# The second MLP of a fused attention-MLP kernel on one core: six token blocks of 384 columns in place of four of 512 and one of 256

## The chip, the core and the metric

The kernel runs on one core of one Trainium2 chip. The metric is device time in microseconds (us) of one execution; lower is better. TensorE (PE) does the matmuls and its weight loads (PEld), ScalarE (ACT) and VectorE (DVE) do the element-wise work, SyncE (SP) issues nearly all DMA transfers, GpSimd (POOL) a few.

## What is computed

Random-feature attention on 4 batches of 8 heads and 576 positions, then two MLPs on its 2304 tokens. The change touches the last one only.

```python
# x: [2304, 512], the attention's result after its heads are put side by side
a = x @ w_a                                   # w_a, w_b: [512, 1536]
b = x @ w_b
y = (a * b) @ w_out                           # w_out: [1536, 512]; first MLP
h = np.maximum(y @ w_in2, 0.0)                # w_in2: [512, 2048]; second MLP
out = (h * h) @ w_out2                        # w_out2: [2048, 512]
```

## The kernel before

**Numbers as two parts.** Every large matmul keeps fp32 accuracy by cutting each operand into a high part and a rest, both in the fp32r format. A product is then three matmuls, by the table `TERMS = ((0, 0), (0, 1), (1, 0))`: high by high, high by rest, rest by high. What an engine produces in fp32 is cut by one cast on ACT (the high part) and one subtraction on DVE (the rest).

**First MLP.** `a_units` goes over the tokens in 9 passes and over the hidden dimension in 12 slices of 128. While its passes run on PE, the attention of later tokens is done beside it (`SIDES`). The result of a pass, transposed (512 features in 4 chunks of 128 partitions, tokens along the free dimension), is scaled by ACT into a tile `y_s` (line 647) and stored to DRAM tensors `y_d`, one for each 512 tokens (line 649). The pool of `y_s` has two buffers.

**Weights of the second MLP.** 16 slices of 128 hidden features. `get_w2` loads one slice of `w_in2` and `w_out2` and cuts both (`split`, lines 151 to 175, some eight instructions on ACT and DVE for each slice). Thirteen slices come in during the last pass of the first MLP; the last three are cut in the first block of the second MLP, in tiles named `w2r`. All 16 then stay on the chip.

**Second MLP.** `BB` lists the token blocks: four of 512 and one of 256 columns. `b_units(i)` does one block. For each hidden slice `f`:

- PE: 12 matmuls `ph` (line 777; 4 chunks of the features by 3 terms) of 128 weights by the block's columns, `yx` streaming;
- ACT: `r` is the scaled relu of `ph` (line 784). DVE: `r` squared (line 785). ACT: the high part of `ss` (line 786). DVE: its rest (line 787);
- PE, one slice later: `outs(f - 1)`, for each tile of 128 tokens three matmuls that stream 512 columns of `w_out2`, with `ss` as the weights, into the bank `o` of that token tile (line 764). So `outs` is 12 matmuls for a block of 512 tokens.

I call `ph` of one slice and `outs` of one slice together a unit. After the last unit, ACT scales each `o` bank into a tile `o_s` (line 796), and SP stores it to the output (line 798). **The pool of `o_s` has two buffers** (line 955): the third `o_s` of a block waits until the store of the first has landed. The next block's relu `r` stands behind these `o_s` in ACT's queue.

`y_load(i)` brings the columns of block `i` back from `y_d`, one feature chunk at a time: a load into `yraw` (line 727; the two buffers of `y_s`), a cast (728) and a subtraction (729) into `yx`. `yx` has one buffer on either side of the memory, used by even and odd blocks, so the load of block `i + 2` can only fill `yx` after the last `ph` of block `i`.

The instructions of one engine run in a fixed order. It comes from the library's scheduler, which places each instruction when its own model of the chip says that the operands are there; the order in the source is only its input. So loads of a later block stand, in the program that runs, at the end of an earlier one.

Of the kernel before, what the change touches and what calls it, by code (L numbers as in the profile page):

```python
# [35 lines left out]
def f32(ap):  # L36
    return ap.bitcast(F32)
# [7 lines left out]
def kernel(  # L45
# [13 lines left out]
    nc = tc.nc  # L59
    B, H, S, D = q.shape  # L60
    M = omega.shape[0]
    NT, DM = out.shape
# [9 lines left out]
    N = 256  # L72
    NBLK = NT // N
# [30 lines left out]
    def bank(i, shape, name):  # L104
# [3 lines left out]
    y_d = [  # L108
        dram.tile([128, KC, min(2, NBLK - i) * N], F32, name=f"y_d{i // 2}")
        for i in range(0, NBLK, 2)  # L110
    ]
# [602 lines left out]

    wi2, wo2 = {}, {}

    BB = [(i * N, min(2, NBLK - i) * N) for i in range(0, NBLK, 2)]
    ys = {}
    op_pool = []

    def y_load(i, pool):
        w_ = BB[i][1]
        t = pool.tile([128, KC, 2, w_], F32R, tag="yx", name=f"yx{i}")
        ys[i] = t
        for c in range(KC):
            r = ypool.tile([128, w_], F32, tag="ys", name="yraw")
            nc.sync.dma_start(out=r, in_=y_d[i][:, c, :])
            nc.scalar.copy(out=t[:, c, 0, :], in_=r)
            nc.vector.tensor_tensor(
                out=t[:, c, 1, :], in0=r, in1=f32(t[:, c, 0, :]), op=ALU.subtract  # L730
            )
# [20 lines left out]
    def b_units(i):  # L752


        y = ys[i]
        c0, w_ = BB[i]
        s_t, op = {}, {}
# [100 lines left out]
    def get_w2():  # L858
        f = w2["n"]
        if f >= FB:  # L860
            return
        w2["n"] += 1
        if f < W2_L:
            po = (w2["l"], "w2")
        elif f < W2_L + FA:
            po = (wpool, "w")
        else:
            po = (w2["r"], "w2r")
        wi2[f], wo2[f] = get_pair(("b", f), 1, *po, (w_in2, f, False), (w_out2, f, True))
# [30 lines left out]
    side, n_side, done, u = iter(()), 0, 0, 0  # L900
# [18 lines left out]
    for pi, f, kind in a_units():  # L919
        _, f0, f1 = PASSES[pi]  # L920
        n_units = (f1 - f0) * 3
        step()
        if kind == "a":
            w_due += W_AT.get(pi, 0) / (f1 - f0)
            while (w_due > 0.999 or w_next <= f + 2 and w_next < f1) and w_next < FA:
                get_w(w_next)
                w_next += 1
                w_due -= 1
        if kind == "o" and (pi or f >= LAG):
            get_wo(n_wo)  # L930
            n_wo += 1
        if pi == last:
            if f == 0 and kind == "o":
                top["st"].close()
                open_split()

            if (f or kind == "o") and w2["n"] < W2_L + f + (kind != "a"):
                get_w2()
            if f == 4 and kind == "o":
                y_load(0, w2["yl"])  # L940
        u += 1
        while done < min(n_side, u * n_side / (n_units * FR.get(pi, 1.0))):
            next(side, None)
            done += 1
        if u == n_units and pi < last:
            begin(pi + 1)
# [8 lines left out]
    op_pool.append(ctx.enter_context(tc.tile_pool(name="op", bufs=2, side="right")))  # L955
    for i in range(len(BB)):
        for f in b_units(i):
            step()
            get_w2()
            if f == (4 if i == 0 else FB - 6) and i + 1 < len(BB):  # L960
                y_load(i + 1, w2["yl" if i % 2 else "yr"])
# [33 lines left out]
```

## Time and profile before

| | us |
|---|---|
| runs: median (lowest to highest) of 3 | 1052.88 (1050.69 to 1053.01) |
| the profiled execution's own time | 1052.61 |
| its span in the profile | 1050.8 |
| PE matmuls busy | 1024.0 (97% of the span) |
| DVE busy | 526.8 (50%) |
| ACT busy | 471.2 (45%) |
| share of PE in the chain that ended last | 88% |
| share of `o` (line 764) and `ph` (line 777) in that chain | 19% and 18% |

The span is what the profile's clock counts from the first to the last instruction; the execution's own time is 1.81 us longer. PE's busy time is built from modelled ends of pipelined matmuls, so a high share alone does not tell at which rate it works; the times from one group of matmuls to the next do.

### The profile page before, as it was taken

How to read it: one execution, taken by the hardware profiler on the slowest of the kernel's cores; microseconds unless marked ns; L12 is line 12 of the kernel's file. 1: busy time of each engine (PE TensorE's matmuls, PEld its weight loads, DVE VectorE, ACT ScalarE, POOL GpSimd, SP SyncE). 2: the span in 40 equal slices, each digit the busy share in tenths (PEclk: the TensorE clock that was granted, in tenths of full speed). 3: DMA queues.
4: the chain of work that ended last, by engine and by line, in shares of the span. 5: the costliest groups of instructions: out<-in, count | busy, mean ns of one | idle time of the engine just before them, and what ended most of it. 6: DMA issues, size and time to landing. Idle time of an engine off the chain costs nothing.

```text
span 1050.8 us, 14948 instructions
## 1 busy us (share of the span) xinstructions
PE 1024.0 (97%) x5641; PEld 873.6 (83%) x5641; DVE 526.8 (50%) x1274; ACT 471.2 (45%) x1079; POOL 28.9 (3%) x54
## 2 busy tenths in 40 slices
PE   4899999999999999999999999999999999999998
PEld 3789989999988877788888888788788888888887
DVE  4788885665654445444337987722222322322222
ACT  4887757554455443333326665522322322322232
POOL 3100101000000000000000000000000000000000
PEclk9999999999999999999999999999999999999999
DMA  6846864663432211312227664300200200100010
GB/s 166 242 148 205 267 233 120 210 209 95 142 105 80 63 46 56 95 62 70 66 87 264 230 220 174 107 1 0 81 1 1 71 1 1 51 1 1 0 41 21
DMA packets 83144, 105.90 MB, mean 101 GB/s; under 512 B 26240, under 2 KB 65152, under 8 KB 83072
## 3 DMA queue, kind: packets, MB, share of 16 engines
q1 hardware_dynamic: 81536, 103.37, 30.7%
q0 software_dynamic: 1536, 1.58, 0.5%
q8 instruction: 45, 0.74, 0.3%
q14 instruction: 27, 0.22, 0.1%
HBM read 87.62 MB, written 17.30 MB: 100 GB/s over the span
## 4 chain that ended last, share of the span: by engine, by line
PE 88%; DVE 4%; DMA 3%; ACT 3%; issue 1%; SPq 1%; ACTq 0%; DVEq 0%
PE abw L610 19%; PE o L764 19%; PE ph L777 18%; PE y L635 12%; PE ab L610 7%; PE ps_n L481 3%; PE ps_p L285 2%; PE ps_kv L423 2%; PE ps_p L351 2%; PE ps_qt L474 1%; DMA raw<-in_moe_w_out_dram 1%; PE ps_t L330 1%; DMA qn<-in_q_dram 1%; DVE p L159 1%; PE ps_x L492 1%
## 5 line engine op out<-in xcount | busy, mean ns | idle before, releaser
L635 PE MATMUL y<-gs,wo 128*128 128x256 f32 (+1 forms) x864 | 177.2, 345 | 0.0
L764 PE MATMUL o<-w,ss 128*128 128x512 f32 x702 | 170.9, 390 | 1.4 <-ACT ss L786 1.4
L777 PE MATMUL ph<-yx,w 128*128 128x512 f32 (+1 forms) x780 | 169.8, 368 | 0.0
L777 PEld LDWEIGHTS ph<-yx,w 128*128 128x128 f32 x780 | 137.4, 188 | 25.3
L785 DVE TENSOR_TENSOR r<-r 128x512 f32<-128x512 f32 (+1 forms) x80 | 51.1, 639 | 209.8 <-ACT r L784 209.8
L764 PEld LDWEIGHTS o<-w,ss 128*128 128x128 f32 x702 | 130.5, 188 | 29.7 <-ACT ss L786 2.2
L635 PEld LDWEIGHTS y<-gs,wo 128*128 128x128 f32 x864 | 136.6, 190 | 15.2
L610 PE MATMUL abw<-x_all,w 128*128 128x512 f32 x576 | 146.6, 398 | 0.0
L784 ACT ACTIVATE r<-ph 128x512 f32<-128x512 f32 (+1 forms) x80 | 44.5, 556 | 208.4 <-PE ph L777 208.2
L610 PE MATMUL ab<-x_all,w 128*128 128x256 f32 x864 | 132.9, 295 | 0.3 <-DVE x_all L549 0.2
L610 PEld LDWEIGHTS abw<-x_all,w 128*128 128x128 f32 x576 | 105.5, 189 | 19.2
L610 PEld LDWEIGHTS ab<-x_all,w 128*128 128x128 f32 x864 | 115.0, 193 | 1.5 <-DVE x_all L549 0.5
L787 DVE TENSOR_TENSOR ss<-r,ss 128x512 fp32r<-128x512 f32 (+1 forms) x80 | 51.1, 639 | 46.6 <-ACT ss L786 40.0
L610 PE MATMUL abw<-x_mid,w 128*128 128x512 f32 x288 | 73.1, 400 | 0.0
L786 ACT CAST ss<-r 128x512 fp32r<-128x512 f32 (+1 forms) x80 | 46.2, 577 | 51.5 <-DVE r L785 51.5
L610 PEld LDWEIGHTS abw<-x_mid,w 128*128 128x128 f32 x288 | 52.1, 189 | 9.8
L358 DVE CUSTOM_DVE_ANT_0 c<-ps_p,c 128x128 f32<-128x128 f32 x152 | 37.8, 287 | 32.5 <-ACT c L356 32.0
L701 ACT CAST gs<-a_s 128x256 fp32r<-128x256 f32 (+1 forms) x96 | 40.6, 433 | 28.3 <-DVE a_s L700 28.1
L164 DVE SCALAR_TENSOR_TENSOR raw<-raw 128x1024 uint32<-128x1024 uint32 (+1 forms) x40 | 42.5, 1062 | 13.4 <-ACT raw L152 13.3
L152 ACT ACTIVATE raw<-raw 128x1024 int32<-128x1024 uint16 (+1 forms) x40 | 40.8, 1020 | 11.4 <-DMA raw<-in_moe_w_out_dram 9.3
L702 DVE TENSOR_TENSOR gs<-a_s,gs 128x256 fp32r<-128x256 f32 (+1 forms) x96 | 42.8, 454 | 5.3 <-ACT gs L701 4.2
L151 ACT ACTIVATE a<-raw 128x1024 f32<-128x1024 f32 (+1 forms) x40 | 40.6, 1014 | 10.9 <-DMA raw<-in_moe_w_out_dram 5.6
(109 smaller groups left out, 1212.9 us busy)
## 6 DMA issues: line engine op xcount, KB each, us to landing
wo<-wo_d SPq DMA_DIRECT2D x60, 512.0 KB, 3.5
raw<-in_moe_w_out_dram SPq DMA_DIRECT2D x28, 512.0 KB, 4.8
raw<-in_moe_w_in_dram SPq DMA_DIRECT2D x16, 512.0 KB, 3.9
raw<-in_moe_w_a_dram SPq DMA_DIRECT2D x12, 512.0 KB, 4.8
raw<-in_moe_w_b_dram SPq DMA_DIRECT2D x12, 512.0 KB, 6.1
wo_d<-wo SPq DMA_DIRECT2D x12, 512.0 KB, 3.4
kn<-in_k_dram SPq DMA_DIRECT2D x16, 256.0 KB, 3.5
V<-in_v_dram SPq DMA_DIRECT2D x16, 256.0 KB, 3.4
```

Source lines behind the costliest of these rows:

```text
L151: nc.scalar.activation(out=a, in_=f32(up), func=ACTF.Copy, scale=WORD_SCALE)
L152: nc.scalar.activation(out=u, in_=raw.bitcast(U16)[:, :, :, 1], func=ACTF.Copy, scale=2.0 ** 7,)
L164: nc.vector.scalar_tensor_tensor(out=u.bitcast(U32), in0=up.bitcast(U32), scalar=23, in1=u.bitcast(U32), op0=ALU.logical_shift_left, op1=A ...
L610: nc.tensor.matmul(ps, lhsT=wv[:, s_, kc, :], rhs=x[..., kc, m_, :], start=(kc == 0 and (s_, m_) == TERMS[0]), stop=(kc == KC - 1 and (s_, ...
L635: nc.tensor.matmul(y_part(pi, f, c), lhsT=wo[pi, f][:, s_, c * 128:(c + 1) * 128], rhs=g[:, m_, :],  start=(f == f0 and (wide or c % 2 == ...
L702: nc.vector.tensor_tensor(out=g[:, 1, c], in0=a_s, in1=f32(g[:, 0, c]), op=ALU.subtract)
L764: nc.tensor.matmul(op[t], lhsT=s_t[f][:, s_, t * 128:(t + 1) * 128], rhs=wo2[f][:, m_, :], start=(f == 0 and (s_, m_) == TERMS[0]), stop=( ...
L777: nc.tensor.matmul(ps, lhsT=wv[:, s_, kc, :], rhs=y[:, kc, m_, :], start=(kc == 0 and (s_, m_) == TERMS[0]), stop=(kc == KC - 1 and (s_, m ...
L784: nc.scalar.activation(out=r, in_=ps, func=ACTF.Relu, scale=1.0 / W_SCALE)
L785: nc.vector.tensor_tensor(out=r, in0=r, in1=r, op=ALU.mult)
L786: nc.scalar.copy(out=s_t[f][:, 0, :], in_=r)
L787: nc.vector.tensor_tensor(out=s_t[f][:, 1, :], in0=r, in1=f32(s_t[f][:, 0, :]), op=ALU.subtract)
```

## The change

The list of blocks becomes six of 384 columns. Since the DRAM tensors `y_d` still hold 512 tokens each, a block's columns may lie in two of them, and its load is then made of two transfers. Nothing else in the source differs; the lines behind it move down by six (777 becomes 783, 796 becomes 802).

```diff
-    BB = [(i * N, min(2, NBLK - i) * N) for i in range(0, NBLK, 2)]
+    NB = 384
+    BB = [(c, NB) for c in range(0, NT, NB)]
...
             r = ypool.tile([128, w_], F32, tag="ys", name="yraw")
-            nc.sync.dma_start(out=r, in_=y_d[i][:, c, :])
+            done = 0
+            while done < w_:
+                d, o = divmod(BB[i][0] + done, 2 * N)
+                cnt = min(w_ - done, 2 * N - o)
+                nc.sync.dma_start(out=r[:, done:done + cnt], in_=y_d[d][:, c, o:o + cnt])
+                done += cnt
```

A block now has three token tiles, so `outs` is 9 matmuls and a unit 12 `ph` of 384 columns and 9 `o` of 512. There are 96 units, where there were 64 of the wide kind and 16 of the narrow kind.

**Where ACT's queue moves: between two blocks.** ACT at the end of the first block of the second MLP, before. Names carry buffer numbers; `o0` to `o3` are the banks of the four token tiles, `o_s` the scaled output tiles, `yx2` the input of the third block.

```order
L784 ACTIVATE r_7736<-ph_7723 128x512
L728 CAST yx2_8111<-yraw_8112 128x512
L728 CAST yx2_8111<-yraw_8116 128x512
L786 CAST ss_7737<-r_7736 128x512
L796 ACTIVATE o_s_7766<-o0_7249 128x512
L796 ACTIVATE o_s_7769<-o1_7253 128x512
L728 CAST yx2_8111<-yraw_8120 128x512
L728 CAST yx2_8111<-yraw_8124 128x512
L796 ACTIVATE o_s_7772<-o2_7257 128x512
L796 ACTIVATE o_s_7775<-o3_7261 128x512
```

The same place with the change.

```order
L790 ACTIVATE r_7697<-ph_7684 128x384
L734 CAST yx2_8032<-yraw_8033 128x384
L734 CAST yx2_8032<-yraw_8038 128x384
L792 CAST ss_7698<-r_7697 128x384
L802 ACTIVATE o_s_7721<-o0_7249 128x512
L802 ACTIVATE o_s_7724<-o1_7253 128x512
L734 CAST yx2_8032<-yraw_8043 128x384
L734 CAST yx2_8032<-yraw_8048 128x384
L802 ACTIVATE o_s_7727<-o2_7257 128x512
```

The fourth `o_s` is gone; the next row is, with the change as before, the next block's first relu. Two `yx` casts and a third `o_s` still stand ahead of it. This holds for the first four of the five places between blocks; at the fifth there are no `yx` casts.

**Where SP's queue moves: the loads.** SP with the change, from the first block's last `ph` on: the loads of `yx2` and the stores of the first two `o_s`. `y_d1` and `y_d2` are DRAM tensors of 512 tokens each.

```order
L732 DMA yraw_8043<-y_d1_98 128x256
L732 DMA yraw_8043<-y_d2_99 128x128
L732 DMA yraw_8048<-y_d1_98 128x256
L732 DMA yraw_8048<-y_d2_99 128x128
L804 DMA out_0_dram<-o_s_7721 128x512
L804 DMA out_0_dram<-o_s_7724 128x512
```

Before, one load of 128x512 stands for each of the two pairs. The block that is loaded at the first place comes in such pairs, and so does the one at the fourth place; at the second and the third each chunk is one load of 128x384.

**Where ACT's queue moves: the start of the second MLP.** Before (`y2`, `y3` are the last results of the first MLP, `w2r` and `raw` belong to weight splits):

```order
L647 ACTIVATE y_s_7179<-y2_6518 128x512
L163 CAST w2r_7226<-p_7266 128x2x512
L647 ACTIVATE y_s_7183<-y3_6519 128x512
L784 ACTIVATE r_7220<-ph_7207 128x512
L152 ACTIVATE raw_7276<-raw_7276 128x1024
L784 ACTIVATE r_7243<-ph_7230 128x512
L786 CAST ss_7221<-r_7220 128x512
```

With the change:

```order
L647 ACTIVATE y_s_7179<-y2_6518 128x512
L790 ACTIVATE r_7220<-ph_7207 128x384
L163 CAST w2r_7226<-p_7262 128x2x512
L647 ACTIVATE y_s_7183<-y3_6519 128x512
L792 CAST ss_7221<-r_7220 128x384
L790 ACTIVATE r_7243<-ph_7230 128x384
```

The first relu moved ahead of the cast of `w2r` and of the last `y_s`, and the first `ss` ahead of a step of a weight split. On PE, 31 matmuls `ph` stand ahead of the first `o` before, and 29 with the change.

## Rows read from the trace of the kernel before

**Rows 1.** Busy time by engine inside the second block; PEclk is the granted clock.

```profile
core 0: us, PE busy (x) PEld busy (x) DVE busy (x) ACT busy (x) POOL busy (x), PEclk, DMA share, GB/s
...
750.00:820.00 70.00, 70.00 (x311) 57.96 (x310) 18.04 (x26) 15.84 (x26) 0.00 (x0) 1.00 0.00 0
```

**Rows 2.** Chain that ended last: a unit of 512 columns (start us, us, what).

```profile
667.98 2.72 PE o L764 x12
670.70 2.72 PE ph L777 x12
```

**Rows 3.** The same chain: a unit of the block of 256 columns.

```profile
1014.43 1.43 PE ph L777 x12
1015.87 1.39 PE o L764 x6
```

**Rows 4.** Groups by shape, weight loads inside the block of 256 columns (busy us, mean ns).

```profile
L777 PEld LDWEIGHTS ph<-yx,w 128*128 128x128 f32 x109 | 14.3, 191 | 0.7
```

**Rows 5.** Groups by shape, ACT and DVE, the whole second MLP.

```profile
L785 DVE TENSOR_TENSOR r<-r 128x512 f32<-128x512 f32 x64 | 44.3, 693 | 184.0 <-ACT r L784 184.0
L784 ACT ACTIVATE r<-ph 128x512 f32<-128x512 f32 x64 | 38.3, 599 | 186.7 <-PE ph L777 186.7
L785 DVE TENSOR_TENSOR r<-r 128x256 f32<-128x256 f32 x16 | 6.8, 426 | 25.9 <-ACT r L784 25.9
L784 ACT ACTIVATE r<-ph 128x256 f32<-128x256 f32 x16 | 6.1, 384 | 21.7 <-PE ph L777 21.6
```

**Rows 6.** Timeline, start of the second MLP (start us, us, engine, line, what, count [idle before]).

```profile
650.26 7.19 PE L777 MATMUL ph<-yx,w 128*128 128x512 f32 x31
...
653.60 0.60 ACT L647 ACTIVATE y_s<-y 128x512 f32<-128x512 f32 x1 [1.32 <-DMA y_d<-y_s]
...
656.20 1.14 ACT L152 ACTIVATE raw<-raw 128x1024 int32<-128x1024 uint16 x1
...
658.38 3.02 PE L764 MATMUL o<-w,ss 128*128 128x512 f32 x12 [0.93 <-ACT ss L786]
```

**Rows 7.** Timeline, from the first to the second block: stores, loads and what waits.

```profile
733.10 5.78 PE L764 MATMUL o<-w2r,ss 128*128 128x512 f32 x24
...
737.08 1.09 ACT L796 ACTIVATE o_s<-o 128x512 f32<-128x512 f32 x2 [1.58 <-PE o L764]
737.70 1.71 SPq L798 DMA_DIRECT2D out_dram<-o_s  x2
...
738.72 5.60 PE L777 MATMUL ph<-yx,w 128*128 128x512 f32 x24
...
740.62 0.62 ACT L728 CAST yx<-yraw 128x512 fp32r<-128x512 f32 x1 [1.43 <-DMA yraw<-y_d]
...
741.79 1.09 ACT L796 ACTIVATE o_s<-o 128x512 f32<-128x512 f32 x2 [0.55 <-DMA out_dram<-o_s]
...
744.79 3.29 PE L764 MATMUL o<-w,ss 128*128 128x512 f32 x12 [0.48 <-ACT ss L786]
```

**Rows 8.** Timeline, the third place between blocks, whose loads are 128x256.

```profile
913.05 4.29 SPq L798 DMA_DIRECT2D out_dram<-o_s  x4
...
915.78 1.20 ACT L796 ACTIVATE o_s<-o 128x512 f32<-128x512 f32 x2 [0.28 <-DMA out_dram<-o_s]
```

**Rows 9.** Timeline, the fourth place, without loads.

```profile
995.89 5.63 PE L764 MATMUL o<-w2r,ss 128*128 128x512 f32 x24
...
999.50 1.29 ACT L796 ACTIVATE o_s<-o 128x512 f32<-128x512 f32 x2 [1.38 <-PE o L764]
1000.13 5.00 SPq L798 DMA_DIRECT2D out_dram<-o_s  x5
...
1002.25 0.60 ACT L796 ACTIVATE o_s<-o 128x512 f32<-128x512 f32 x1 [1.45 <-DMA out_dram<-o_s]
```

**Rows 10.** Timeline, the end of the program.

```profile
1043.90 3.26 PE L764 MATMUL o<-w2r,ss 128*128 128x512 f32 x12
...
1047.12 1.03 SPq L798 DMA_DIRECT2D out_dram<-o_s  x2
```

## The prediction, made before the changed kernel ran

> **What bounds the kernel now.** I read the chain that ended last first: it is PE for 88%, and from the start of the second MLP it shows nothing but `o` and `ph` in turn, 2.72 us for each group of 12 matmuls of 512 columns [rows 2]. That is 226.7 ns for one matmul. Next I asked whether anything else presses: inside a block PE is busy for 70.00 of 70.00 us at a granted clock of 1.00, which is the 2.4 GHz level, while DVE and ACT work 18.0 and 15.8 us of them and no bytes move [rows 1]. So inside a block PE's own pace is the bound, and everything else is covered. The timeline then shows where PE does wait: at the start of the second MLP [rows 6], and between blocks [rows 7 to 9]. The reader is to see in rows 7 that the third `o_s` waits for the first store to land, and that the next block's first `o` waits for what stands behind that `o_s` on ACT. The end of the program is a fixed tail: last matmuls, `o_s`, store [rows 10].
>
> So the change is costed in three parts: PE's work, PE's waits, the tail. I use the profiled execution: 1052.61 us, 0.27 below the median of the three runs; its span is 1050.8.
>
> **PE's work.** Before, a wide unit is 5.44 us [rows 2] and a narrow one 1.43 + 1.39 = 2.82 us [rows 3]; 64 of the one and 16 of the other make 348.2 + 45.1 = 393.3 us. With the change `outs` streams the same 512 columns for the same 18 token tiles, 864 matmuls as before: no saving. `ph` streams as many columns in all, in 96 × 12 = 1152 matmuls where there were 80 × 12 = 960. No row has 384 columns. The bounds are 119.2 ns for 256 columns [rows 3] and 226.7 ns for 512 [rows 2]; the two lie on a line of 2.4 columns to the nanosecond plus some 13 ns for each matmul, and its middle is 173 ns. A unit is then 12 × 173 + 9 × 226.7 ns = 4.12 us, 96 of them 395.1 us. Beside short groups an `o` group took 1.39 us for 6, which is 0.03 over the wide rate; half of that in each of 96 units would make 396.5. I take 395.5: **2.2 us more work**, between 1.8 and 3.2.
>
> A rule of the Trainium skill says how much a finer cut costs. The page "TensorE: Matmul & The Clock Gate", section Back-to-back issue gap, gives columns over 2.4 GHz plus about 2.5 ns as the gap of matmuls one behind another at the full clock. As an estimate from that page, 192 more matmuls would cost 0.5 us and the sum below would be 1.7 us lower. The trace does not agree, with some 13 ns over the columns' time at both sizes [rows 2, 3], and the sum goes by the trace.
>
> ACT and DVE do 96 small rounds instead of 80. At 384 columns I put `r` at 0.49 us and its square at 0.56, midway in rows 5, and the cast like `r`. One slice's chain, some 2.2 us, is covered by the `outs` and `ph` that lie between, 4.1 us. Cost nothing; without that cover it would be 2 us a unit.
>
> **PE's waits, before.** The first `ph` starts at 650.26 [rows 6] and the last matmul ends at 1043.90 + 3.26 = 1047.16 [rows 10]: 396.9 us for 393.3 of work, so 3.6 us of waits in all, 0.93 of it at the start [rows 6].
>
> **Waits between blocks.** Let T be the start of the last `outs` of a block. At the first place T = 733.10 + 2.72 = 735.82 [rows 7]. The first `o_s` starts at T + 1.26, its store is issued at T + 1.88, and the third `o_s` starts at T + 5.97, 4.09 us after the issue. From it to the next block's first `o` are 3.00 us, 0.49 of it the fourth `o_s` (two take 1.09, one 0.60). PE could have gone on at T + 2.72 + 5.44 = T + 8.16 and went on at T + 8.97.
>
> With the change PE comes to the same point earlier: T + 2.04 + 4.15 = T + 6.19. ACT's order is the same but for the fourth `o_s`. From the third `o_s` to the first `o` I count 3.00 − 0.49, less 0.11 + 0.13 + 0.11 for the shorter relu, square and cast [rows 5], which is 2.16 us. Let w be the time from the first store's issue to the third `o_s`. PE then waits 1.88 + w + 2.16 − 6.19 = w − 2.15 us. The rows give w = 4.09 beside loads of 512 columns [rows 7], 2.73 beside loads of 256 [rows 8], 2.12 beside none [rows 9]. For 384 columns I take the middle of the first two, 3.4, since load size orders these three: a wait of 1.3 us. That is for the second and third place.
>
> At the first and fourth place the loads come in two pieces. The last of them is issued two issues later, of some 0.5 us each [rows 10], and its cast stands ahead of the third `o_s`. Before, that cast began at T + 4.80 [rows 7]; about 0.9 later it ends near T + 6.2, and PE would wait 6.2 + 2.16 − 6.19 = 2.2 us. The smaller bytes pull the other way; I take 2.0. The fifth place has no loads: w = 2.12, no wait. Sum **6.6 us** (2 × 1.3 + 2 × 2.0). The ends: nothing, if w is 2.12 everywhere; 9.3, with 4.09 everywhere and 0.8 more for the pieces.
>
> **Waits at the start.** 29 `ph` take 5.0 us, so PE is done with them at 655.3, where 31 had taken it to 657.45 [rows 6]. The first `ss` now stands ahead of a split step of 1.14 us and of the second relu, 0.49; with the shorter relu and cast the first `o` comes at about 658.38 − 1.14 − 0.49 − 0.2 = 656.55. The wait is 1.3 us, for 0.93. After it ACT and DVE still owe the splits of two weight slices and the loads of the second block, at units that last 4.12 us instead of 5.44; I add 0.7 for this. Together 2.0, between 0.9 and 3.0. With 0.3 of remains, the waits come to 2.0 + 6.6 + 0.3 = 8.9, **5.3 more than before**.
>
> **The tail.** Before, the last block had two tiles for two `o_s` buffers, so nothing waited. Now its third `o_s` waits for its first store. From T of the last block: first `o_s` at T + 0.89 (999.50 less 995.89 + 2.72) and store at T + 1.52 [rows 9], landed 2.12 later, third `o_s` at T + 3.64, its store at T + 4.26. Before, the second store was issued at the end of the `o_s`, 3.0 us ahead of the span's end [rows 10]; so the span ends at T + 7.3, that is 5.2 us behind the last matmul (T + 2.04), where it was 1050.8 − 1047.16 = 3.6: **1.6 us more**, between 1.2 and 2.4.
>
> **Sum.** 1052.61 + 2.2 + 5.3 + 1.6 = 1061.7 us, 0.8% slower.
>
> **The rivals.**
>
> *The stores land undisturbed (no change).* With smaller loads and one `o_s` less, the first store might land 2.12 us after its issue at every place, as in rows 9. It decides at w = 2.15: below it ACT is ready before PE and the places between blocks cost nothing. If the start also stays at 0.93, the waits fall by 2.4 and the time is 1052.61 + 2.2 − 2.4 + 1.6 = 1054.0. For it: the one place without loads. Against it: w was over 2.7 at each of the places with loads [rows 7, 8], and four of five places still have them.
>
> *Weight loads set the pace of `ph`.* A load is 191 ns on average [rows 4] and a matmul of 384 columns would be 173. If loads bound it, 1152 × 18 ns = 20.7 us come on top: 1082.4. Against it: the same loads stand beside matmuls that follow each other every 119 ns [rows 3], so they overlap one another.
>
> *PE's clock falls behind longer waits.* The wait of 0.93 us [rows 6] and those between blocks left the clock at its upper level. Waits of 2 us or more could bring a stretch at 1.2 GHz, where a unit would take 8.24 us; one such unit behind each of four places costs 4 × 4.12 = 16.5 us: 1078.2. Nothing in the rows shows such a fall in this MLP. The Trainium skill's page "TensorE: Matmul & The Clock Gate", section Why this matters for your kernels, warns that pauses between bursts of matmuls bring back the half clock.
>
> **How the numbers follow.** The forecast has 0.87, the undisturbed stores 0.08, the weight loads 0.02, the clock 0.03. About 0.3% is what a measurement of this kernel can tell from no change, 3.2 us on 1052.88. The forecast's bounds: the places between blocks alone reach from 0 to 9.3 us around 6.6, work, start and tail add about 1 us to either side. Its likely part is 1056.5 to 1066.5; the first rival lies just below, the other two far above, and together they are less than 2 in 10, so the range stays at that. Slower by over 0.3% takes the forecast and the last two rivals, 0.92; no change takes the first rival, 0.07, and 0.01 of it is left for faster.
>
> **What would show each step.** In the changed profile: groups of 12 `ph` at 2.08 us (a group near 2.3 would mean weight loads); the first `o` of blocks two to five some 1.3 to 2 us late, with a third `o_s` that waits for the store just ahead of it, and the last block without that wait; the granted clock at 1.00 in every block; a third `o_s` at the end that starts about 2.1 us behind the first store. The prediction is wrong if PE goes from one block to the next without a wait, or if the waits between blocks exceed 3 us each.

## The result, and the profile after

| | before | with the change |
|---|---|---|
| median of 4 runs each, us (lowest to highest) | 1051.89 (1050.69 to 1053.01) | 1063.13 (1061.44 to 1065.62) |
| ratio to before, 95% interval | | 1.0109 (1.0082 to 1.0136) |
| profiled execution: own time / span, us | 1052.61 / 1050.8 | 1065.62 / 1063.8 |

The change costs 1.1%, within the range that was forecast. But two of its three terms were wrong, one far too small and one far too large, and they made up for each other. The profile shows which.

First the chain that ended last, inside the second block (start us, us, what); it answers to [rows 2].

```profile
740.35 2.10 PE ph L783 x12
742.45 2.08 PE o L770 x9
744.54 2.10 PE ph L783 x12
```

A unit is 4.19 us, where I had put 4.12. Now the busy times of the same block, which answer to [rows 1]:

```profile
core 0: us, PE busy (x) PEld busy (x) DVE busy (x) ACT busy (x) POOL busy (x), PEclk, DMA share, GB/s
735.00:780.00 45.00, 45.00 (x229) 40.85 (x228) 12.00 (x22) 10.56 (x21) 0.00 (x0) 1.00 0.00 1
```

PE shows no idle time there, and its clock is at the upper level, 2.4 GHz. So the 0.07 us lie between matmuls that follow each other without a wait. The timeline at the fourth place between blocks, which answers to [rows 7]:

```profile
919.25 4.44 PE L770 MATMUL o<-w2r,ss 128*128 128x512 f32 x18
...
921.27 0.54 PEld L770 LDWEIGHTS o<-w2r,ss 128*128 128x128 f32 x3 [0.22 <-ACT ss L792]
...
922.04 1.21 PEld L770 LDWEIGHTS o<-w2r,ss 128*128 128x128 f32 x6 [0.23 <-DVE ss L793]
922.59 1.09 ACT L802 ACTIVATE o_s<-o 128x512 f32<-128x512 f32 x2 [1.36 <-PE o L770]
923.21 4.07 SPq L804 DMA_DIRECT2D out_dram<-o_s  x3
923.52 4.35 PE L783 MATMUL ph<-yx,w 128*128 128x384 f32 x24
...
925.40 0.51 ACT L734 CAST yx<-yraw 128x384 fp32r<-128x384 f32 x1 [0.72 <-DMA yraw<-y_d]
...
926.32 0.60 ACT L802 ACTIVATE o_s<-o 128x512 f32<-128x512 f32 x1 [0.41 <-DMA out_dram<-o_s]
...
928.49 2.35 PE L770 MATMUL o<-w,ss 128*128 128x512 f32 x9 [0.62 <-ACT ss L792]
```

The chain of events is the forecast one: the third `o_s` waits for the first store, behind it comes the next block's first relu, and the first `o` is late. This is the worst of the five places. Counted from PE's pace, the first `o` comes 0.78 us late there (the 0.62 in the last row counts from the modelled end of `ph`); I had put 2.0. And the end, which answers to [rows 10]:

```profile
1054.27 4.40 PE L770 MATMUL o<-w2r,ss 128*128 128x512 f32 x18
...
1057.33 1.29 ACT L802 ACTIVATE o_s<-o 128x512 f32<-128x512 f32 x2 [1.18 <-PE o L770]
1057.96 3.24 SPq L804 DMA_DIRECT2D out_dram<-o_s  x3
1060.24 0.60 ACT L802 ACTIVATE o_s<-o 128x512 f32<-128x512 f32 x1 [1.62 <-DMA out_dram<-o_s]
```

The third `o_s` starts 2.28 us behind the issue of the first store, where the forecast had 2.12, and the span ends 5.18 us behind the last matmul (1054.27 + 4.40 = 1058.67).

The stretch that the change touches runs from the first `ph` to the end of the span: 1050.8 − 650.26 = 400.54 us before, 1063.85 − 652.67 = 411.18 with the change, 10.6 more.

| part of that stretch, us | before | with the change | more | forecast |
|---|---|---|---|---|
| units at their own pace (with the change 96 × 4.187) | 393.3 | 402.0 | 8.7 | 2.2 |
| the rest up to the last matmul | 3.6 | 4.0 | 0.4 | 5.3 |
| behind the last matmul | 3.64 | 5.18 | 1.5 | 1.6 |

The other 2.4 us of the two profiled executions lie ahead of it, in a part that the change leaves alone. The granted clock there, first of the kernel before, then with the change:

```profile
core 0: us, PE busy (x) PEld busy (x) DVE busy (x) ACT busy (x) POOL busy (x), PEclk, DMA share, GB/s
50.00:54.00 4.00, 3.17 (x21) 2.66 (x21) 1.99 (x3) 3.79 (x8) 0.00 (x0) 1.00 1.08 309
54.00:60.00 6.00, 4.92 (x34) 4.12 (x33) 5.45 (x9) 5.75 (x17) 0.00 (x0) 1.00 0.53 177
```

```profile
50.00:54.00 4.00, 2.56 (x18) 1.98 (x15) 1.99 (x3) 3.55 (x5) 0.00 (x0) 0.94 0.97 313
54.00:60.00 6.00, 5.03 (x20) 4.17 (x19) 4.53 (x8) 5.21 (x16) 0.00 (x0) 0.50 0.37 124
```

With the change PE did 20 matmuls at 1.2 GHz in six microseconds where before it did 34 at 2.4; ahead of that it had been busy for 2.56 of 4 us, and before for 3.17. The mean clock of the four runs with the change was 0.995, 1.000, 0.998 and 0.999, so this differs from run to run. How much of the 2.4 us the clock made was not separated: in the profiles of this case the first `ph` starts anywhere from 647.5 to 654.6 us. Therefore the experiments are compared by the stretch from the first `ph` on, and their medians stand beside it. A second profile of the changed kernel gave 410.94 us for it, beside 411.18.

### The profile page after: what moved, and what is told of

Same layout as the page of the kernel before. It is cut to its first block, busy times and chain, and to the rows that moved or that the text cites. A ratio compares the mean times of both kernels' runs of the same rounds, so it can differ in the third digit from the quotient of the medians.

```text
span 1063.8 us, 15478 instructions
## 1 busy us (share of the span) xinstructions
PE 1035.3 (97%) x5833; PEld 910.5 (86%) x5833; DVE 531.8 (50%) x1310; ACT 478.3 (45%) x1115; POOL 29.5 (3%) x54
## 4 chain that ended last, share of the span: by engine, by line
PE 86%; DMA 5%; DVE 4%; ACT 3%; issue 1%; SPq 0%; ACTq 0%; DVEq 0%
PE o L770 19%; PE abw L610 18%; PE ph L783 17%; PE y L635 12%; PE ab L610 7%; PE ps_n L481 3%; PE ps_p L285 2%; PE ps_p L351 2%; PE ps_kv L423 2%; DMA raw<-in_moe_w_b_dram 2%; DMA raw<-in_moe_w_out_dram 2%; PE ps_qt L474 1%; PE ps_t L330 1%; DMA out_dram<-o_s 1%; DVE p L159 1%
## 5 line engine op out<-in xcount | busy, mean ns | idle before, releaser
L770 PE MATMUL o<-w,ss 128*128 128x512 f32 x702 | 175.7, 394 | 2.1 <-ACT ss L792 1.9
L783 PE MATMUL ph<-yx,w 128*128 128x384 f32 x936 | 175.8, 336 | 0.0
L783 PEld LDWEIGHTS ph<-yx,w 128*128 128x128 f32 x936 | 166.1, 188 | 6.3
L791 DVE TENSOR_TENSOR r<-r 128x384 f32<-128x384 f32 x96 | 53.6, 558 | 210.8 <-ACT r L790 210.8
L790 ACT ACTIVATE r<-ph 128x384 f32<-128x384 f32 x96 | 47.2, 492 | 210.6 <-PE ph L783 210.4
L793 DVE TENSOR_TENSOR ss<-r,ss 128x384 fp32r<-128x384 f32 x96 | 53.6, 558 | 50.0 <-ACT ss L792 49.3
L792 ACT CAST ss<-r 128x384 fp32r<-128x384 f32 x96 | 49.2, 513 | 54.6 <-DVE r L791 54.6
L164 DVE SCALAR_TENSOR_TENSOR raw<-raw 128x1024 uint32<-128x1024 uint32 (+1 forms) x40 | 42.5, 1062 | 12.6 <-ACT raw L152 12.4
```

Source lines behind the costliest of these rows:

```text
L164: nc.vector.scalar_tensor_tensor(out=u.bitcast(U32), in0=up.bitcast(U32), scalar=23, in1=u.bitcast(U32), op0=ALU.logical_shift_left, op1=A ...
L770: nc.tensor.matmul(op[t], lhsT=s_t[f][:, s_, t * 128:(t + 1) * 128], rhs=wo2[f][:, m_, :], start=(f == 0 and (s_, m_) == TERMS[0]), stop=( ...
L783: nc.tensor.matmul(ps, lhsT=wv[:, s_, kc, :], rhs=y[:, kc, m_, :], start=(kc == 0 and (s_, m_) == TERMS[0]), stop=(kc == KC - 1 and (s_, m ...
L790: nc.scalar.activation(out=r, in_=ps, func=ACTF.Relu, scale=1.0 / W_SCALE)
L791: nc.vector.tensor_tensor(out=r, in0=r, in1=r, op=ALU.mult)
L792: nc.scalar.copy(out=s_t[f][:, 0, :], in_=r)
```

## The experiments

**Where the 0.07 us of a unit lie.** The trace's start times, in ns from one matmul to the next, read in a steady unit of each kind:

```
with the change   o  (512)  229 233 236 224 231 236 228 233 231
                  ph (384)  171 175 177 185 176 182 173 174 173 173 174 173
before, wide      o  (512)  227 226 227 227 226 227 227 226 227 227 226 227
before, narrow    o  (512)  233 236 228 233 230 227
                  ph (256)  113 120 120 120 120 120 120 120 120 120 120 120
```

The settled paces are 120.0, 173.3 and 226.7 ns, which is 288, 416 and 544 cycles of 2.4 GHz: the columns plus 32. So the line through [rows 2, 3] was right. But a group whose size differs from the one ahead does not run at its pace at once: `o` behind `ph` of 384 columns is irregular over all its 9 matmuls, 41 ns above its pace in sum, and `ph` behind `o` over its first 6, 26 ns above. The pattern is the same, to 2 ns, in the units in which PE does not wait. Theory: a change of the streamed size costs. Rivals: ACT and DVE, which work during just these matmuls, or the tiles' addresses, which now lie at multiples of 384.

**One size for both.** `o` streams only 384 of its columns; the last 128 output columns are left out.

```diff
-                    op[t] = bank(t, [128, DM], f"o{t}")
+                    op[t] = bank(t, [128, 384], f"o{t}")
...
-                        op[t], lhsT=s_t[f][:, s_, t * 128:(t + 1) * 128], rhs=wo2[f][:, m_, :],
+                        op[t], lhsT=s_t[f][:, s_, t * 128:(t + 1) * 128], rhs=wo2[f][:, m_, 0:384],
...
-            nc.scalar.mul(out=o, in_=op[t], mul=1.0 / W_SCALE)
+            nc.scalar.mul(out=o[:, 0:384], in_=op[t], mul=1.0 / W_SCALE)
+            nc.scalar.copy(out=o[:, 384:DM], in_=op[t][:, 0:128])
```

> Blocks of 384, but o streams only 384 of its 512 columns, so ph and o have one size (the last 128 output columns are left out of the sum and filled with copies). With the change a unit measured 4.187 us where the columns and 13.3 ns for each matmul make 4.12; the missing 67 ns lie in the first half of ph and in all of o. Theory, the change of size: going from one streamed size to another costs, so without it all 21 matmuls follow each other at 173.3 ns, a unit takes 3.64 us, and the whole is some 50 us shorter than the change (1010 to 1015 us). Rival, contention with ACT and DVE: their work is as before, so the 67 ns stay, and a unit takes 3.70 to 3.71 us, 6.4 us more in all (1017 to 1021).

1014.55 us. The chain, in the third block:

```profile
816.93 2.08 PE ph L783 x12
819.01 1.56 PE o L770 x9
820.57 2.08 PE ph L783 x12
```

3.64 us, and in these steady units every interval is 173 or 174 ns. The same `ss`, the same `yx`, the same work beside, and no irregular matmul is left there: the addresses of `ss` and `yx` and the work beside do not make it, since they are unchanged.

**Nothing beside PE.** The element-wise steps are done for one slice of each block only, and all `o` use that slice (the others' sums are left out).

```diff
-            r = gp.tile([128, w_], F32, tag="t", name="r")
-            s_t[f] = gp.tile([128, 2, w_], F32R, tag="gs", name="ss")
-            nc.scalar.activation(out=r, in_=ps, func=ACTF.Relu, scale=1.0 / W_SCALE)
...
+            if f:
+                s_t[f] = s_t[0]
+            else:
+                r = gp.tile([128, w_], F32, tag="t", name="r")
+                s_t[f] = gp.tile([128, 2, w_], F32R, tag="gs", name="ss")
+                nc.scalar.activation(out=r, in_=ps, func=ACTF.Relu, scale=1.0 / W_SCALE)
...
```

> Blocks of 384; relu, square, cast and rest are done for the first slice of a block only and o uses that one for all slices (the others' sums are left out). So ACT and DVE are idle inside a block. Theory, the change of size: ph 2.10 to 2.11 us for 12, o 2.08 for 9, a unit stays at 4.187 us. Rival, contention with ACT and DVE: a unit falls to 4.12 us and the whole by 6 us.

1058.22 us, stretch 408.98. Busy times and chain:

```profile
735.00:780.00 45.00, 45.00 (x228) 40.86 (x227) 0.53 (x2) 0.93 (x2) 0.00 (x0) 1.00 0.00 1
```

```profile
806.21 2.10 PE ph L783 x12
808.32 2.08 PE o L770 x9
810.40 2.10 PE ph L783 x12
```

DVE and ACT work 0.5 and 0.9 us of 45, and the unit is 4.19 us as with the change. Contention with ACT and DVE is out. The stretch is 2.2 us shorter because PE's waits, mostly those between the blocks, fall from 4.2 to 2.1 us.

**Half as many changes of size.** Two slices at a time.

```diff
-            s_t[f] = gp.tile([128, 2, w_], F32R, tag="gs", name="ss")
+            s_t[f] = ss_pool[0].tile([128, 2, w_], F32R, tag="ss", name="ss")
...
-            if f:
+            if f % 2:
+                if f > 1:
+                    outs(f - 2)
                 outs(f - 1)
...
+    ss_pool.append(ctx.enter_context(tc.tile_pool(name="ssp", bufs=3, side="right")))
```

> Blocks of 384, two slices at a time: 24 ph, then 18 o, with three buffers for ss. Half as many changes of size, the same matmuls. Theory, the change of size: ph loses 26 ns once per pair, o 41 to 82, so two slices take 8.31 to 8.35 us instead of 8.37, 1.2 to 3.2 us less work in all. Rivals, the tiles' addresses or ACT and DVE beside PE: 8.37 us as before. The waits between blocks may grow, since the first o of a block comes as early as before; 1059 to 1064 us beside 1063 for the change.

Median 1060.44 us, ratio to before 1.0084 (1.0062 to 1.0105); stretch 408.46, 2.7 less than the change.

```profile
802.50 4.18 PE ph L784 x24
806.68 4.12 PE o L771 x18
810.80 4.18 PE ph L784 x24
```

Two slices take 8.31 us instead of 8.37 (4.18 + 4.12 in the rows, 8.307 from the start times). In a group of 24 the first six intervals are those shown above and the other 18 are 173 or 174; in one of 18 the first nine are irregular and the other nine 226 or 227. So the cost belongs to the change of size, once for each change: 67 ns for the two of a unit, 6.4 us for 96 units. The 192 more matmuls are 192 × 13.3 ns = 2.6. Less the 0.3 us that the changes of size in the 16 narrow units cost before (20 ns each: `o` 27 above its pace, `ph` 7 below), that makes the 8.7 us. PE's waits grew by 0.3 us in all: the first `o` comes 1.25 and 0.97 us late at the first two places, where it had been 0.29 and 0.22, and is no longer late at the fourth.

**All blocks of 256.**

```diff
-    NB = 384
+    NB = 256
```

> Nine blocks of 256. All units are of the narrow kind that the kernel before had 16 of. Theory, the change of size with 32 cycles for each matmul: 12 ph in 1.43 us, 6 o in 1.39, 144 units of 2.82 make 406.1 us of PE work, 4.2 more than the change. With two token tiles for two o_s buffers no o_s waits for a store, so the end is as in the kernel before (3.6 us behind the last matmul) and the waits between blocks come only from the yx casts: first ph to end 411 to 417 us beside 411.1 with the change, 1062 to 1068 us. Rival, a fixed cost per block: eight places between blocks at the 0.4 us each that the change shows, and units dearer than 2.82; over 418 us.

Median 1068.93 us, ratio to before 1.0154 (1.0130 to 1.0178); stretch 417.3, just above the expected 411 to 417.

```profile
803.35 1.43 PE ph L783 x12
804.78 1.39 PE o L770 x6
806.17 1.43 PE ph L783 x12
```

The units are the 2.82 us that were worked out, and the end behind the last matmul is 3.76 us, as it should be with two tiles for two buffers. Up to the last matmul it is 413.5 us for 406.1 of units: 7.4 us of waits, just above the 1.3 to 7.3 that the expected stretch leaves for them. Counted from PE's pace, 2.5 us lie at the start, 0.3 in the last `outs` of the program, and 0.6 at each of the eight places, about half of it in the last `outs` of the block and half at the first `o` of the next. A cause was not tested; at both, only one or two short groups of matmuls stand between a slice's `ph` and its `outs`. The median lies just above the expected 1062 to 1068 as well.

**A third buffer for `o_s`.**

```diff
-    op_pool.append(ctx.enter_context(tc.tile_pool(name="op", bufs=2, side="right")))
+    op_pool.append(ctx.enter_context(tc.tile_pool(name="op", bufs=3, side="right")))
```

> Blocks of 384, three buffers for o_s instead of two. Theory: the third o_s no longer waits for the first store. At the end the third store is issued some 1.3 us earlier, and the first o of blocks two to five comes without the waits of the changed kernel (2.15 us for the five places together), so 2.5 to 3.5 us less. Rival, ACT's queue is held by the yx casts and not by the store: the waits between blocks stay, only the 1.3 us at the end go.

Median 1058.88 us, ratio to before 1.0073 (1.0051 to 1.0095); stretch 407.64, 3.5 less than the change. The fourth place again, and the end:

```profile
912.94 4.46 PE L770 MATMUL o<-w2r,ss 128*128 128x512 f32 x18
...
916.28 1.75 ACT L802 ACTIVATE o_s<-o 128x512 f32<-128x512 f32 x3 [1.36 <-PE o L770]
...
917.24 4.35 PE L783 MATMUL ph<-yx,w 128*128 128x384 f32 x24
...
921.43 2.31 PE L770 MATMUL o<-w,ss 128*128 128x512 f32 x9
...
1050.31 1.97 ACT L802 ACTIVATE o_s<-o 128x512 f32<-128x512 f32 x3 [1.18 <-PE o L770]
1050.94 1.70 SPq L804 DMA_DIRECT2D out_dram<-o_s  x3
```

The three `o_s` follow each other, and `o` comes where PE is ready for it (917.24 + 4.35 = 921.59, less the modelled overlap). The end falls from 5.18 to 3.69 us, and 2.05 us go from between the blocks and the start, 0.24 of them at the start, which the edit leaves alone. Two `yx` casts still stand ahead of the next relu, and the wait is gone; the buffer was the cause between the blocks and at the end.

**Both edits.** Two slices at a time and three buffers.

> Blocks of 384 with both of the edits tried alone: two slices at a time, and three buffers for o_s. Alone they took the stretch from the first ph to the end of the span from 411.1 to 408.4 and 407.6 us. Theory, two separate causes: they add up, 404.5 to 405.5 us, and what is left over the kernel before's 400.5 is the 192 more matmuls (2.6 us) and half of the changes of size. Rival, one shared cause: 407 us or more.

Median 1055.50 us, ratio to before 1.0030 (1.0017 to 1.0044); stretch 404.08. The two gains alone, 2.7 and 3.5 us, make 404.9 if added, and 404.5 to 405.5 was expected. So there are two causes, as expected, but together they give 0.8 us more than added: beside pairs the third buffer saves 2.9 us of PE's waits, and alone 2.1.

**The store beside the loads.** w is the time from the issue of the first store to the third `o_s`. Without loads (the third to the sixth block take the inputs of the first two; their columns are left out):

```diff
         w_ = BB[i][1]
+        if i > 1:
+            ys[i] = ys[i - 2]
+            return
```

> Blocks of 384; the third to the sixth block take the inputs of the first two instead of loading their own (their columns are left out), so no loads stand between the blocks. w is the time from the issue of the first store to the third o_s; the changed kernel showed 2.64, 2.57, 2.84, 3.11 and 2.12 us at its five places, the last without loads. Theory, loads beside the store lengthen it: w is 2.1 to 2.2 at all five, and PE hardly waits between blocks. Rival, the yx casts on ACT are what the third o_s waits for: the same outcome in time, but then w in the other runs would follow the casts' ends and not the landing of the store.

With loads of 512 columns for the fourth and fifth block, twice:

```diff
-            r = ypool.tile([128, w_], F32, tag="ys", name="yraw")
-            done = 0
+            d0, o0 = divmod(BB[i][0], 2 * N)
+            wide_l = o0 + w_ <= 2 * N and d0 < len(y_d) - 1
+            if wide_l:
+                r_ = ypool.tile([128, 2 * N], F32, tag="ys", name="yraw")
+                nc.sync.dma_start(out=r_, in_=y_d[d0][:, c, :])
+                r = r_[:, o0:o0 + w_]
+            else:
+                r = ypool.tile([128, w_], F32, tag="ys", name="yraw")
+            done = w_ if wide_l else 0
```

Each of the first four places has two chunks of one block ahead of its first store, and the first three have chunks of the next block behind it. So the edit widens loads behind the store at the first place, on both sides of it at the second, and ahead of it at the third. (It also widens the first block's loads, long before.)

> Blocks of 384, but the loads at the second and third place between blocks bring 512 columns for each feature chunk (the outer ones are not used), 256 KB in place of 192. In the changed kernel the third o_s starts 2.57 and 2.84 us behind the issue of the first store there. Theory, bytes: load size orders this time, as the prediction read it, so it rises towards the 4.1 us that the kernel before showed beside such loads, at least to 3.4, and the first o of blocks three and four comes 0.6 to 1.5 us later. Rival, position: in the changed kernel the loads are issued earlier against the store than before, so the time changes by no more than 0.3 us.

> The loads of 512 columns once more. The first time w was 2.57 at the second place and 3.65 at the third. Bytes: 3.4 or more at both. Position: within 0.3 us of 2.57 and 2.84, so the 3.65 was one slow transfer. If the third place alone is again above 3.4, it is that place's order of issues.

And the changed kernel once more:

> The changed kernel once more. If w belongs to the place, it comes within 0.2 us of 2.64, 2.57, 2.84, 3.11 and 2.12; if it varies from run to run, as the transfers' own times do, the places with loads differ by 0.3 us or more while the one without stays at 2.1.

| w at the five places, us | 1 | 2 | 3 | 4 | 5 |
|---|---|---|---|---|---|
| the change | 2.64 | 2.57 | 2.84 | 3.11 | 2.12 |
| once more | 2.55 | 2.47 | 2.89 | 3.08 | 2.11 |
| without loads | 2.31 | 2.26 | 2.49 | 2.20 | 2.11 |
| loads of 512 columns | 2.62 | 2.57 | 3.65 | 2.87 | 2.10 |
| the same, again | 2.64 | 2.82 | 3.37 | 2.71 | 2.10 |

Each w is read from two rows, here the third place without loads and then with loads of 512 columns the second time:

```profile
851.93 3.45 SPq L807 DMA_DIRECT2D out_dram<-o_s  x3
854.42 0.60 ACT L805 ACTIVATE o_s<-o 128x512 f32<-128x512 f32 x1 [1.83 <-DMA out_dram<-o_s]
```

```profile
853.17 0.82 SPq L811 DMA_DIRECT2D out_dram<-o_s  x2
...
856.54 0.60 ACT L809 ACTIVATE o_s<-o 128x512 f32<-128x512 f32 x1 [1.10 <-DMA out_dram<-o_s]
```

These four runs are single ones; their times were 1060.95 us without loads, 1060.88 and 1063.47 with loads of 512 columns, 1067.31 for the changed kernel once more, above the four runs of the result; its profile shows the early stretch at 1.2 GHz again. Their stretches are 408.58, 411.50, 411.46 and 410.94 us.

Without loads w falls by 0.2 to 0.9 us at the four places that had them. It does not fall to the expected 2.1 to 2.2 at all of them: 2.20 to 2.49 are left, so the places differ with stores alone. In the changed kernel w belongs to the place, for the repeat differs by at most 0.1; with loads of 512 columns two runs differ by up to 0.28. Bytes alone do not set it. A third more of them added 0.5 to 0.8 us at the third place and 0 to 0.35 at the second, and the 4.1 us of the kernel before was not reached. Neither expectation held at both places. What makes the places differ was not settled; the order in which loads and stores are issued differs between them and was not varied by itself.

**The kernel before without its waits for stores.** Its third and fourth `o_s` go to a scratch tile.

```diff
-            o = op_pool[0].tile([128, DM], F32, tag="o", name="o_s")
+            if t < 2:
+                o = op_pool[0].tile([128, DM], F32, tag="o", name="o_s")
+            else:
+                if t == 2:
+                    o2 = top["cut"].tile([128, 2, 512], F32, tag="p", name="o_s2")
+                o = o2[:, t - 2]
```

> The kernel before the change, with the third and fourth o_s of a block in a scratch tile of the weight splits, which is free by then, so that no o_s waits for a store. Theory: of the 3.6 us of PE's waits in the second MLP the part between blocks goes, 1.5 to 2 us, and all else stays; first ph to end of the span 398.5 to 399 us instead of 400.5, ratio 0.998 to 0.999, which the times alone may not tell from 1. Rival: the yx casts hold ACT as long as the store did, and the stretch stays at 400 to 400.5.

Median of 12 runs 1051.17 us beside 1052.28 of 23 runs of the kernel before; ratio 0.9990 (0.9977 to 1.0003). The stretch is 398.84 us instead of 400.54. Of the 1.7 us, 1.2 went between the blocks, somewhat less than the expected 1.5 to 2, and 0.5 at the start, which the edit leaves alone (PE's wait there is 0.7 to 1.2 us in the profiles of the kernel before and of blocks of 384). The times cannot tell the gain from nothing. The place that answers to [rows 7]:

```profile
735.61 1.09 ACT L801 ACTIVATE o_s<-o 128x512 f32<-128x512 f32 x2 [1.57 <-PE o L764]
...
737.25 5.60 PE L777 MATMUL ph<-yx,w 128*128 128x512 f32 x24
737.70 1.08 ACT L801 ACTIVATE o_s<-o 128x512 f32<-128x512 f32 x2
...
742.68 2.91 PE L764 MATMUL o<-w,ss 128*128 128x512 f32 x12
```

The two later `o_s` start 2.1 us behind the first pair, where they had started 4.7 behind, and the first `o` has no idle time ahead of it.

## Why the prediction was right in sum and wrong in two terms

**PE's work: the mechanism was right, the size was not.** I gave "2.2 us more work", between 1.8 and 3.2; it measured 8.7. The 192 more matmuls cost what the line through two sizes said (2.6 us, 13.3 ns each). The step that failed is the sentence on `o` groups beside short ones: they "took 1.39 us for 6, which is 0.03 over the wide rate", and I took half of that as an upper bound. That 0.03 was no remainder. It was the change of size, paid by each of the 16 narrow units, and with 384 columns every unit pays it, 41 ns at `o` and 26 at `ph`. Taken whole it would still have given less than half of the 6.4 us, since no row of the kernel before has 384 columns beside 512. I had averaged the group, so a cost of the border looked like a slightly slower rate; and I let a steady pace, read in units of one size, stand for units of two.

**PE's waits: the mechanism was right, the size was not.** Forecast 5.3 more, measured 0.4. The formula w − 2.15 gives 0.49, 0.42, 0.69, 0.96 and 0 us at the measured w; the first `o` came 0.29, 0.22, 0.49, 0.78 and 0 us late. So it is 0.2 us too high: PE came to that point at T + 6.39 and not at T + 6.19. Two thirds of this are two waits of 0.07 us for `ss` inside the last `outs` of a block (the two PEld rows at the fourth place), which I had put at nothing; there no `ph` lies between to cover the chain. The rest are the changes of size. With w − 2.35 the formula fits to 0.03 us, also in the runs with loads of 512 columns. The step that failed is w itself: 3.4 us from a line through load sizes, 2.57 and 2.84 measured at the two places meant. Load size does not order it: 2.57 beside loads of 384 columns is less than the 2.73 beside loads of 256 before. The surcharge for loads in two pieces was wrong as well: w is 2.64 and 3.11 there, and the piece's cast was never what ended the wait: at the four places ACT is idle for 0.39 to 1.18 us between the last cast and the third `o_s`. What sets w instead stays open. At the start PE waits 1.1 us, counted from its pace, as before; the 0.7 us for the owed splits did not appear.

**The tail: right.** Forecast 1.6 more, measured 1.5; the third buffer took all of it back.

**The rivals.** Stores that land undisturbed: w was 2.6 to 3.1 with loads, over the 2.15 at which that rival decides, so no; but the waits came out nearer to it than to the forecast. Weight loads as the bound of `ph`: one takes 188 ns in the changed profile, and the settled pace is 173.3. The clock: 1.00 in the whole second MLP; PE waits 0.8 us at most between blocks and 1.1 us at the start. The Trainium skill (the page "TensorE: Matmul & The Clock Gate", section Back-to-back issue gap) gives about 2.5 ns over the columns' time, and calls it the gap of an isolated matmul; I had put it to a stream. The settled pace of this kernel does not agree with it at any of the three sizes: 13.3 ns, constant, and the measured number decides.

So the forecast for the stretch, 409.6 us, came within 1.6 us of the measured 411.2 because +6.5 and −4.9 met; that was luck. Had the waits been priced right, the forecast would have been 1057.

## What to carry to other kernels

When a loop alternates matmuls of two streamed sizes, read a whole period of the group that follows the change, matmul by matmul; the pace of a steady stretch and the mean of a group both hide what the border costs. A cut into smaller blocks cost one fixed overhead per matmul (13.3 ns here) plus one border per group, whose price depends on the two sizes (67 ns for both borders of 384 and 512 columns, 20 ns for 256 and 512); longer groups of one size won back part of the second. And where a block has one more tile than its output pool has buffers, the next block and the program's end wait for a store: one buffer removed both here.

## What the runs showed that I had not expected

After some changes of its size a stream of matmuls needs five to nine matmuls to settle, with a fixed pattern of intervals (224 to 236 ns for 512 columns behind 384, where the settled pace is 226.7). Afterwards it keeps its pace to the trace's nanosecond: 120.0, 173.3 and 226.7 ns, the columns plus 32 cycles of 2.4 GHz. In the kernel before, a wait inside a wide group is followed by such a pattern too (236, 228, 233, 231, then 226 and 227 again). What in the engine causes it was not found. From 512 down to 256 columns there is none beyond the first interval of 113 ns, so it depends on the two sizes.
